# A first layer with half passes, a shorter lead, and f32 products in the last units

## The chip, the cores and the metric

The kernel runs on one core of one Trainium2 chip. The metric is the device time of a run in microseconds (us); lower is better. The engines are TensorE (PE in the profile; PEld is its weight load), VectorE (DVE), ScalarE (ACT), GpSimd (POOL) and SyncE (SP), which here only starts transfers.

## The reference, cut to what matters

```python
X = real(fft(fft(x, axis=1), axis=2))        # x: 8 x 3072 x 256 f32 -> 24576 tokens of 256
logits = X @ w_gate                          # 8 experts
e = argmax(logits, axis=1); gate = softmax(logits)[e]
ye = maximum(X @ w1[e], 0.0) @ w2[e]         # w1 256 x 1024, w2 1024 x 256, for each expert
X = gate * ye
h = X @ w_in                                 # 256 x 2048
P = a[0] + a[1]*h + a[2]*h**2 + a[3]*h**3
Q = 1.0 + abs(b[0])*abs(h) + abs(b[1])*h**2
out = (P / (Q + 1e-06)) @ w_out              # 2048 x 256, f32, 24576 x 256
```

With the inputs drawn, the experts get 3033, 3287, 3143, 2830, 2990, 2942, 3351 and 3000 tokens.

## The kernel before, in words

Three stages follow one another on the core.

*Transform, gate, scatter* (to about 350 us of the span). The two Fourier transforms are matrix products. Each token's expert, its place in that expert's list and its gate are found, and GpSimd scatters the token's row into `xs` in DRAM, sorted by expert (`scatter`, L610, 128 rows per indirect transfer). From the counts, VectorE computes tables for the first layer: which expert each pass has (`ej`), at which row its tokens start (`offi`), where its weights lie (`widx`), and a scale for each pass (`rj`, L990 to L993).

*First layer.* 103 passes (`NSB`) of 256 tokens, ordered by expert; each expert has as many whole passes as its tokens need. A pass loads 256 rows of `xs` (`load`, L1145), scales them and splits them into two f16 halves (`pairs`, L1151), transposes them (`transp`, L1167: on PE in the first ten passes, by DMA later), and has four pieces: `m1a` twice (the product with `w1`, 24 matmuls of 256 columns each, then ReLU on ACT and the rest of the f16 split on VectorE) and `m1b` twice (the product with `w2`, 24 matmuls). The weights of two passes lie in `wslot[0]` and `wslot[1]`; `gather` (L1004, an indirect transfer of 2 MB on POOL) loads them for pass j + 2, and moves nothing where the expert is the same. The result goes to `ys` in DRAM, in the sorted order, and the tokens' numbers to `idd`.

*Second layer.* 96 blocks of 256 tokens, four rational units each; the last unit is cut into two of half the width, so there are 385. A unit (j, u) has `m2a` (24 matmuls with `w_in`, then Abs, Square and Identity on ACT and the numerator, two operations, on VectorE: L1310 to L1315), `m2b` (Ln and Exp on ACT, L1322 and L1324, for the reciprocal of Q, and three operations on VectorE, L1325 to L1327), `m2g` (the product as two 16-bit halves `ghi` on ACT, L1335, and `glo` on GpSimd, L1336) and `m2c` (24 matmuls with `w_out`, L1348, into `po`; after a block's last unit it is scaled and scattered to the output). `bound_sum`, `bound`, `bound_scale` and `bound_out` work out scales for each block; `load_y` loads a block of `ys`.

The order of the work is written by hand: each engine runs its instructions in the order in which the code issues them. Lead: `np_` = 36 pieces without units, and beside each a `step` of a generator that prepares `w_in` and `w_out` (decode on VectorE, splits on ACT and GpSimd). Then one turn per unit i: `m2b` of unit i − 1, `m2a` of unit i, the piece i + `np_`, `m2g`, and `m2c` of unit i − 3. On PE that is m2a, a piece and m2c, three groups of 24 matmuls. Units 0 to 375 have a piece beside them; behind `free` = 4 · 103 − 36 = 376 there is none left.

## Time and profile before

| | us |
|---|---|
| median of 3 runs | 3513.91 (3513.57 to 3516.85) |
| profiled execution | 3516.32 |
| its span | 3514.6 |
| PE busy | 3391.1 (96%) |
| ACT busy | 3123.4 (89%) |
| DVE busy | 3044.7 (87%) |
| POOL busy | 2824.1 (80%) |

The span runs from the first to the last recorded instruction; 1.7 us of the profiled execution lie outside it. The mean granted clock of TensorE was 0.984 of full speed. The shares are averages over stages: in a table by windows, or in the chain of waits, each stage shows which engine sets its pace.

### The profile page before, as it was taken

What the parts mean: (1) busy time and instruction counts of PE and PEld (TensorE: products, weight loads), DVE (VectorE), ACT (ScalarE), POOL (GpSimd) and SP (SyncE); (2) the same over time, 40 slices, a digit from 0 to 9 for tenths busy, and PEclk for the clock granted to TensorE, in tenths of its full rate; (3) what the DMA queues carried; (4) which work ended last, traced back from release to release, by engine and by line L of the source; (5) the groups of instructions that cost most, each with busy time, mean ns of one, the idle gap of its engine ahead of it and who ended that gap; (6) DMA issues with size and microseconds to landing.
All of it is one profiled execution on the core that took longest, in us unless ns stands there. A gap on an engine that the chain in (4) does not pass through costs nothing.

```text
span 3514.6 us, 75025 instructions
## 1 busy us (share of the span) xinstructions
PE 3391.1 (96%) x29902; PEld 2968.8 (84%) x29902; DVE 3044.7 (87%) x3214; ACT 3123.4 (89%) x3904; POOL 2824.1 (80%) x2552
## 2 busy tenths in 40 slices
...
DMA packets 344639, 268.32 MB, mean 76 GB/s; under 512 B 182470, under 2 KB 319686, under 8 KB 337232
## 3 DMA queue, kind: packets, MB, share of 16 engines
...
q10 hardware_dynamic: 128, 1.06, 0.1%
...
## 4 chain that ended last, share of the span: by engine, by line
PE 88%; DVE 4%; ACT 2%; issue 2%; DMA 2%; POOL 1%; POOLq 0%; SPq 0%; ACTq 0%; DVEq 0%
PE po L1348 28%; PE h L1189 14%; PE h L1188 14%; PE h L1191 14%; PE py L1191 5%; PE py L1188 5%; PE py L1189 5%; POOL xs L612 1%; DMA xs<-y,sli 1%; PE ps L507 1%; PE pq L531 1%; PE ps L480 1%; PE pq L532 1%; DVE h L1326 0%; ACT h L1324 0%
## 5 line engine op out<-in xcount | busy, mean ns | idle before, releaser
L1188 PE MATMUL h<-yr,win 128*128 128x256 f16 x3072 | 755.7, 273 | 8.9 <-DVE u__5102 L1327 5.6
L1189 PE MATMUL h<-yr,win 128*128 128x256 f16 x3072 | 755.7, 273 | 0.0
L1348 PE MATMUL po<-wout,ghi 128*128 128x256 f16 x6144 | 735.1, 273 | 11.2 <-ACT ghi L1335 7.6
L1348 PEld LDWEIGHTS <-ghi 128*128 128x128 f16 x6144 | 593.6, 98 | 81.7 <-ACT ghi L1335 12.0
L1191 PE MATMUL h<-yr,win 128*128 128x256 f16 x3072 | 587.5, 273 | 0.0
L1324 ACT ACTIVATE h<-L,bnd 128x1024 f32<-128x1024 f32 x385 | 429.6, 1116 | 20.9 <-DVE u__47829 L1315 1.5
L1188 PE MATMUL h<-xt,wslot 128*128 128x256 f16 x1648 | 406.3, 274 | 2.5 <-DVE hlo L1214 1.7
L1189 PE MATMUL h<-xt,wslot 128*128 128x256 f16 x1648 | 406.3, 274 | 0.0
L1348 PE MATMUL po<-wout,glo 128*128 128x256 f16 x3072 | 399.3, 273 | 1.8 <-POOL glo L1336 1.8
L1188 PE MATMUL py<-hhi,wslot 128*128 128x256 f16 x1648 | 373.4, 274 | 3.5 <-ACT hhi L1208 3.5
L1189 PE MATMUL py<-hhi,wslot 128*128 128x256 f16 x1648 | 373.3, 274 | 0.0
L1189 PEld LDWEIGHTS <-wslot 128*128 128x128 f16 x3296 | 323.5, 98 | 45.1 <-issue 6.9
L1188 PEld LDWEIGHTS <-wslot 128*128 128x128 f16 x3296 | 323.3, 98 | 39.1 <-issue 0.4
L1191 PEld LDWEIGHTS <-wslot 128*128 128x128 f16 x3296 | 323.1, 98 | 38.5 <-issue 0.3
L1188 PEld LDWEIGHTS <-win 128*128 128x128 f16 x3072 | 300.7, 98 | 45.5 <-DVE u__5102 L1327 5.7
L1348 PEld LDWEIGHTS <-glo 128*128 128x128 bf16 x3072 | 300.4, 98 | 38.4 <-POOL glo L1336 3.2
L1189 PEld LDWEIGHTS <-win 128*128 128x128 f16 x3072 | 301.0, 98 | 35.2
L1191 PEld LDWEIGHTS <-win 128*128 128x128 f16 x3072 | 300.8, 98 | 35.2
L612 POOL DMA_INDIRECT xs<-y,sli x192 | 225.5, 1175 | 117.1 <-ACT L L535 58.5
L1191 PE MATMUL h<-xt,wslot 128*128 128x256 f16 x1648 | 315.8, 273 | 0.0
L1214 DVE SCALAR_TENSOR_TENSOR hlo<-h,hhi 128x1024 f16<-128x1024 f32 x197 | 240.0, 1218 | 29.1 <-ACT hhi L1208 24.1
L1361 POOL DMA_INDIRECT out_dram<-o,id x192 | 199.3, 1038 | 53.7 <-issue 47.3
...
## 6 DMA issues: line engine op xcount, KB each, us to landing
xr<-xs SPq DMA_DIRECT2D x103, 258.0 KB, 2.9
ys<-yw SPq DMA_DIRECT2D x103, 256.0 KB, 5.5
yr<-ys SPq DMA_DIRECT2D x96, 256.0 KB, 3.8
...
ws<-wh SPq DMA_DIRECT2D x16, 1024.0 KB, 12.1
...
```

The costliest lines, as they stand in the source:

```text
L480: nc.tensor.matmul(ps[0:m, 0:n], lhsT=eo[i][:, jh, c], rhs=mat[:, c, 0:n], start=c == 0, stop=c == 2)
L507: nc.tensor.matmul(ps[q][0:m, 0:NH], lhsT=eo[i][:, c], rhs=mat[:, c], start=c == 3 * q, stop=c == 3 * q + 2)
L531: nc.tensor.matmul(pq[:, k, 0:NC], lhsT=u[2 * par][:, js], rhs=rc, start=True, stop=False)
L532: nc.tensor.matmul(pq[:, k, 0:NC], lhsT=u[2 * par + 1][:, js], rhs=rs, start=False, stop=True)
L612: ins = nc.gpsimd.indirect_dma_start(out=xs, out_offset=bass.IndirectOffsetOnAxis(ap=sli[:, t0 + t:t0 + t + 1], axis=0), in_=y[:, t], in_o ...
L1188: nc.tensor.matmul(ps, lhsT=wa[i], rhs=xa[i], start=i == 0, stop=False)
L1189: nc.tensor.matmul(ps, lhsT=wb[i], rhs=xa[i], start=False, stop=False)
L1191: nc.tensor.matmul(ps, lhsT=wa[i], rhs=xb[i], start=False, stop=i == n - 1)
L1214: V.scalar_tensor_tensor(out=hlo[:, sl], in0=ps, scalar=0.0, in1=hhi[:, sl], op0=ALU.max, op1=ALU.subtract)
L1324: nc.scalar.activation(out=ps, in_=L, func=AF.Exp, scale=-1.0, bias=st["bnd", j][3])
L1348: nc.tensor.matmul(ps[:, q], lhsT=g[:, f - fs[0], q * P:(q + 1) * P], rhs=wout[:, h, 4 * u + f], start=g is ghi and u == 0 and f == 0 and ...
L1361: ins = nc.gpsimd.indirect_dma_start(out=out, out_offset=bass.IndirectOffsetOnAxis(ap=t[:, q:q + 1], axis=0), in_=o[:, q], in_offset=None, ...
```

## The change

1. The first layer gets `NF` = 95 passes of 256 tokens and nine *half passes* of 128. The tables for the half passes come from `half_tables`, run in three bursts in the turns of units 6, 14 and 22. A half pass has two pieces: `half_a` (48 matmuls of 128 columns) and both halves of `m1b` (48 matmuls of 128 columns). Where a pass of 256 tokens took four turns, a half pass takes two.
2. The lead has 24 pieces, with three steps of the preparation for two pieces. PE transposes serve the first 7 passes instead of 10. `load_y(0)` and the first bounds move along.
3. The load of the second weight slot and the operations for `rj` move behind the first loads of `xs`; the first pass is split by the gate scale in one operation per half instead of a multiply, a copy and a subtract; the edge tile scatters 8 rows instead of 128.
4. The units without a piece (375 to 384, `late`) issue `m2a` with `m2b` of the unit before between their own operations: Identity, the numerator, Abs, then `m2b`, then Square. Their product stays f32: no `ghi` and `glo`, and `m2c` has 8 matmuls in f32 with `w_out` widened to f32 into `wslot[0]` (`widen`).
5. `bound_sum` and `bound` run in turn u = 2 of a block instead of u = 1 where half passes stand (`at`).

The core of the diff:

```diff
+HB = TB // 2
...
-    NSB = NT // TB + E - 1
+    NF = NT // TB - 1
+    NSB = NF + E + 1
...
-        scatter(ye, sli, 0)
+        scatter(ye, sli, 0, B)
...
-        v = nc.sync.value_load(widx[0:1, 1:2], min_val=0, max_val=(E - 1) * P)
-        for h in range(2):
-            c = slice(4096 * h, 4096 * h + 4096)
-            nc.sync.dma_start(out=wslot[1][:, c], in_=ws[ds(v, P), c])
...
-        V.tensor_tensor(out=prod, in0=ej.unsqueeze(2).to_broadcast(bl),
-                        in1=sm[:, 8:16].unsqueeze(1).to_broadcast(bl), op=ALU.is_equal)
-        V.tensor_tensor(out=prod, in0=prod, in1=kk.unsqueeze(1).to_broadcast(bl), op=ALU.mult)
-        V.tensor_reduce(out=rj, in_=prod, axis=AX.X, op=ALU.add)
...
+    def full_scales():
+
+        bl = [P, NF, E]
+        t = tp.tile([P, 4, TB], F32, tag="u", name="rt").rearrange("p f t -> p (f t)")[:, 0:NF * E]
+        t = t.rearrange("p (j e) -> p j e", e=E)
+        V.tensor_tensor(out=t, in0=ej[:, 0:NF].unsqueeze(2).to_broadcast(bl),
+                        in1=sm[:, 8:16].unsqueeze(1).to_broadcast(bl), op=ALU.is_equal)
+        V.tensor_tensor(out=t, in0=t, in1=kk.unsqueeze(1).to_broadcast(bl), op=ALU.mult)
+        V.tensor_reduce(out=rj[:, 0:NF], in_=t, axis=AX.X, op=ALU.add)
...
+    def half_tables():
+
+        n = NSB - NF
...
+    def load_second(h):
+        c = slice(4096 * h, 4096 * h + 4096)
+        if h == 0:
+            st["w"] = nc.sync.value_load(widx[0:1, 1:2], min_val=0, max_val=(E - 1) * P)
+        nc.sync.dma_start(out=wslot[1][:, c], in_=ws[ds(st["w"], P), c])
...
+        if j == 0:
+            for i in range(n):
+                nc.scalar.activation(out=xp[:, i, 0], in_=t[:, i, 0:D], func=AF.Copy, scale=gs[:, i:i + 1])
+            for i in range(n):
+                V.scalar_tensor_tensor(out=xp[:, i, 1], in0=t[:, i, 0:D], scalar=gs[:, i:i + 1], in1=xp[:, i, 0],
+                                       op0=ALU.mult, op1=ALU.subtract)
...
-        if j < E + 2:
+        if j < LAG + 2:
...
+    def half_a(j):
+
+        W = wslot[j % 2]
+        xhi, xlo = [t[:, :, 0:HB] for t in st["xs", j]]
+        hhi = bp.tile([P, 8, TB], F16, tag="hhi", name="hhi")[:, :, 0:HB]
+        hlo = bp.tile([P, 8, TB], F16, tag="hlo", name="hlo")[:, :, 0:HB]
+        st["h", j] = (hhi, hlo)
+        ps = psM.tile([P, 4, TB], F32, tag="h1", name="h1").rearrange("p f (a t) -> p (f a) t", t=HB)
+        for f in range(8):
+            fo = f * P
+            three(ps[:, f], [W[:, kc * F1 + fo:kc * F1 + fo + P] for kc in range(2)],
+                  [W[:, 2048 + kc * F1 + fo:2048 + kc * F1 + fo + P] for kc in range(2)],
+                  [xhi[:, kc] for kc in range(2)], [xlo[:, kc] for kc in range(2)])
+        nc.scalar.activation(out=hhi, in_=ps, func=AF.Relu)
+        V.scalar_tensor_tensor(out=hlo, in0=ps, scalar=0.0, in1=hhi, op0=ALU.max, op1=ALU.subtract)
...
+        st["r", j, u, fs] = (ps, sq_, u_)
+
+        def numerator():
+            V.tensor_tensor(out=u_, in0=u_, in1=ps, op=ALU.mult)
+            V.scalar_tensor_tensor(out=u_, in0=u_, scalar=ka1, in1=ps, op0=ALU.add, op1=ALU.mult)
+
+        if between is not None:
+            nc.scalar.activation(out=u_, in_=ps, func=AF.Identity, scale=ka3, bias=ka2)
+            numerator()
         nc.scalar.activation(out=ab_, in_=ps, func=AF.Abs, scale=kb0)
+        if between is not None:
+            between()
         nc.scalar.activation(out=sq_, in_=ps, func=AF.Square, scale=kb1)
-        nc.scalar.activation(out=u_, in_=ps, func=AF.Identity, scale=ka3, bias=ka2)
+        if between is None:
+            nc.scalar.activation(out=u_, in_=ps, func=AF.Identity, scale=ka3, bias=ka2)
         (V if fs[0] else nc.gpsimd).tensor_tensor(out=sq_, in0=sq_, in1=ab_, op=ALU.add)
-        V.tensor_tensor(out=u_, in0=u_, in1=ps, op=ALU.mult)
-        V.scalar_tensor_tensor(out=u_, in0=u_, scalar=ka1, in1=ps, op0=ALU.add, op1=ALU.mult)
-        st["r", j, u, fs] = (ps, sq_, u_)
...
+    w32 = wslot[0].bitcast(F32)
+
+    def widen(q):
+        nc.gpsimd.tensor_tensor(out=w32[:, 1024 * q:1024 * q + 1024].rearrange("p (k d) -> p k d", d=D),
+                                in0=wout[:, 0, 4 * q:4 * q + 4], in1=wout[:, 1, 4 * q:4 * q + 4], op=ALU.add)
+
     def m2g(j, u, fs=range(4)):
         ps, q_, w_ = st.pop(("r", j, u, fs))
+        if 4 * j + u > free:
+            st["g", j, u, fs] = (w_, None)
+            return
...
+        if glo is None:
+            for f in fs:
+                k = (4 * u + f) * D
+                for q in range(2):
+                    nc.tensor.matmul(ps[:, q], lhsT=ghi[:, f - fs[0], q * P:(q + 1) * P], rhs=w32[:, k:k + D],
+                                     start=u == 0 and f == 0 and q == 0, stop=u == 3 and f == 3,
+                                     skip_group_check=True)
+        for g, parts in ((ghi, (0, 1)), (glo, (0,))) if glo is not None else ():
...
+        if i < 4 * NF:
+            j, s_ = divmod(i, 4)
+        else:
+            j, s_ = NF + (i - 4 * NF) // 2, (i - 4 * NF) % 2
+            if j >= NSB:
+                return
+            if s_ == 0:
+                pairs(j + 1, 1)
+                half_a(j)
+                if j + 1 < NSB:
+                    transp(j + 1)
+                if j + 3 < NSB:
+                    load(j + 3)
+            else:
+                m1b(j, 0, False)
+                m1b(j, 1, False)
+                pairs(j + 2, 0)
+                if j + 2 < NSB:
+                    gather(j + 2)
...
+    NB = NT // TB
+    LAG = E // 2 + 1
+    np_ = 24
+    free = 4 * NF + 2 * (NSB - NF) - np_
...
+    load_second(0)
     load_words(3, raw_in[1])
+    load_second(1)
...
+    gather(0)
     side = prologue()
+    late_tables = half_tables()
...
+    full_scales()
     load_words(5, raws[1])
 
-    NB = NT // TB
-    LAG = E
-    np_ = 4 * LAG + 4
     for i in range(np_):
-        if i == 4 * LAG:
+        if i == np_ - 4:
             load_y(0)
-        if i == 4 * LAG:
             bound_rows(0)
         piece(i, True)
-        step(1)
-        if i > 4 * LAG:
-            (bound_sum, bound, bound_scale)[i - 4 * LAG - 1](0)
+        step(2 - i % 2)
+        if i > np_ - 4:
+            (bound_sum, bound, bound_scale)[i - np_ + 3](0)
...
+    def at(i):
+        return 1 if i - i % 4 + 1 + np_ < 4 * NF else 2
...
+        late = free < i < len(units)
+        if 1 <= i <= len(units) and not late:
             m2b(*units[i - 1])
-        if i == len(units) - 1:
-            m2g(*units[i - lag])
         if i < len(units):
             j, u = units[i][:2]
             if i == 0:
                 piece(np_)
-            m2a(*units[i])
+            m2a(*units[i], between=(lambda: m2b(*units[i - 1])) if late else None)
             if i < len(units) - 1:
                 if i:
                     piece(i + np_)
-                if u == 1 and j + 1 < NB:
+                if u == at(i) and j + 1 < NB:
                     bound_sum(j + 1)
                 if u == 3 and j + 1 < NB:
                     bound_scale(j + 1)
                 if u == 1 and j + 1 < NB:
                     load_y(j + 1)
-        if i not in (free + 1, len(units) - 1, len(units)) and lag <= i < len(units) + lag:
+        if i not in (free + 1, len(units)) and lag <= i < len(units) + lag:
             m2g(*units[i - lag])
+        if free <= i < free + 4:
+            widen((i + 1) % 4)
...
+        if i % 8 == 6:
+            next(late_tables, None)
```

Two places show what moves in the engines' order, the first on two engines. On ScalarE, from the first units after the last piece. `ab`, `sq`, `u`, `L` and `h` are tiles of a unit, with a number for each; before:

```order
L1322 ACTIVATE L<-sq__47210,c1b 128x1024 [waits Pool_49]
L1324 ACTIVATE h_47184<-L,bnd 128x1024 [waits DVE_49,Activation_49]
L1310 ACTIVATE ab__47325<-h_47300,coef 128x1024 [waits PE_49]
L1311 ACTIVATE sq__47326<-h_47300,coef 128x1024
L1312 ACTIVATE u__47327<-h_47300,coef 128x1024
```

and now, for the unit with `h_47505` and the unit before it with `h_47436`:

```order
L1422 ACTIVATE u__47532<-h_47505,coef 128x1024 [waits PE_49]
L1424 ACTIVATE ab__47530<-h_47505,coef 128x1024 [waits DVE_49]
L1438 ACTIVATE L<-sq__47462,c1b 128x1024 [waits Pool_49]
L1440 ACTIVATE h_47436<-L,bnd 128x1024 [waits Activation_49]
L1427 ACTIVATE sq__47531<-h_47505,coef 128x1024
```

Abs (L1424) stands behind Identity and waits for VectorE; Exp (L1440) no longer does. On VectorE, in the same place of the changed program (the numerator is L1418 and L1419; L1441 to L1443 are those of `m2b`):

```order
L1441 SCALAR_TENSOR_TENSOR u__47389<-u__47389,a_3464,h_47362 128x1024 [waits Activation_49]
L1442 SCALAR_TENSOR_TENSOR h_47362<-sq__47388,h_47362 128x1024 [waits Pool_49]
L1443 SCALAR_TENSOR_TENSOR u__47389<-h_47362,bnd,u__47389 128x1024 [waits DVE_49]
L1418 TENSOR_TENSOR u__47532<-u__47532,h_47505 128x1024 [waits Activation_49]
L1419 SCALAR_TENSOR_TENSOR u__47532<-u__47532,coef,h_47505 128x1024 [waits DVE_49]
```

The value that Abs of `h_47505` waits for on VectorE is that of the last of these rows, the numerator of the same unit, and ahead of it stand the three operations of an earlier unit (`h_47362`). The other place is SyncE at the end of the scatter stage. Before, the two loads of the second weight slot (`wslot_70`; TENSOR_LOAD and ISA rows read an address for a transfer) stand ahead of the first load of `xs`:

```order
L951 DMA wslot_70<-ws 128x4096 [waits DMAHW4_49,DMAHW3_49,PE_49]
L951 ISA
L951 DMA wslot_70<-ws 128x4096 [waits DMAHW4_49,PE_49]
L1148 DMA xr<-xs 128x2x258 [waits DMASW4_49,DMASW5_49,DMASW3_49,DMASW6_49,DMASW2_49,DMASW7_49,DMASW1_49,DMAHW5_49,DMASW0_49,DMAHW7_49,DVE_49,Activation_49]
L1146 TENSOR_LOAD offi [waits DVE_49]
```

and now they stand behind the three loads of `xr`, of which the last is shown:

```order
L1218 DMA xr<-xs 128x2x258
L1224 TENSOR_LOAD widx
L1224 ISA x2
L1225 ISA
L1225 DMA wslot_70<-ws 128x4096
L225 DMA xh_68<-in_moe_w_in_dram 128x2048 [waits DVE_49]
```

The load of the slot no longer shares the transfer engines with the last scatters, and shares them with the loads of the word tiles `xh`.

## Rows read from the trace of the kernel before

**Rows 1.** The page, busy time of each engine, its share of the span and instructions.

```profile
PE 3391.1 (96%) x29902; PEld 2968.8 (84%) x29902; DVE 3044.7 (87%) x3214; ACT 3123.4 (89%) x3904; POOL 2824.1 (80%) x2552
```

**Rows 2.** Windows: length, busy time of the engines (instructions), granted clock, DMA share, GB/s.

```profile
2000.00:3000.00 1000.00, 1000.00 (x9210) 895.91 (x9209) 890.09 (x828) 945.25 (x1082) 839.34 (x766) 1.00 0.24 56
3485.00:3492.00 7.00, 5.53 (x27) 3.92 (x28) 5.68 (x6) 6.40 (x8) 6.51 (x5) 0.53 0.11 39
```

**Rows 3.** The chain of waits, 1000 to 1040 us: start, us, engine, tile and line.

```profile
1005.54 2.62 PE po L1348 x24
...
1013.40 2.62 PE po L1348 x24
```

**Rows 4.** The chain of waits at the boundary, 326 to 362 us.

```profile
343.88 5.78 DMA xs<-y,sli
...
352.86 0.70 DVE xr L1160
...
356.38 0.37 PE h L1188
```

**Rows 5.** Timeline of VectorE at the boundary: start, us, line, operation.

```profile
341.72 1.01 DVE L990 TENSOR_TENSOR blk<-tri,sm 128x832 f32<-128x832 f32 x1
...
343.82 1.02 DVE L993 TENSOR_REDUCE rj<-blk 128x104 f32<-128x832 f32 x1
```

**Rows 6.** Timeline of SyncE's queue, 336 to 338 us.

```profile
336.60 1.53 SPq L951 DMA_DIRECT2D wslot<-ws  x2
```

**Rows 7.** Timeline of PE at the end of the lead, 470 to 475 us.

```profile
474.43 0.27 PE L1188 MATMUL h<-yr,win 128*128 128x256 f16 x1
```

**Rows 8.** Waits of PE in the lead: total us, times, longest.

```profile
PE py L1188 <- ACT hhi L1208: 3.5, 2, 2.5
```

**Rows 9.** DMA issues in the lead: count, KB each, median us to landing.

```profile
wslot<-ws,widx POOLq DMA_INDIRECT x9, 10.8
```

**Rows 10.** The page, DMA issues of the whole span.

```profile
ys<-yw SPq DMA_DIRECT2D x103, 256.0 KB, 5.5
yr<-ys SPq DMA_DIRECT2D x96, 256.0 KB, 3.8
```

**Rows 11.** Timeline of PE, 364.4 to 365.2 us: transposes of 128 columns.

```profile
364.48 0.61 PE L1177 MATMUL pt<-ident,xp 128*128 128x128 f16 x8
364.93 0.27 PE L1188 MATMUL py<-hhi,wslot 128*128 128x256 f16 x1
```

**Rows 12.** Weight loads by line and shape: busy us, mean ns of one.

```profile
L1348 PEld LDWEIGHTS <-ghi 128*128 128x128 f16 x6144 | 593.6, 98 | 81.7 <-ACT ghi L1335 12.0 <-issue 0.9
```

**Rows 13.** Timeline of PE in the transform stage: f32 matmuls of 273 columns.

```profile
286.44 0.62 PE L531 MATMUL pq<-wslot,u 128*128 128x273 f32 x2
286.90 0.63 PE L532 MATMUL pq<-wslot,u 128*128 128x273 f32 x2
```

**Rows 14.** Timeline of ScalarE in the tail.

```profile
3419.96 1.12 ACT L1324 ACTIVATE h<-L,bnd 128x1024 f32<-128x1024 f32 x1
...
3450.63 1.12 ACT L1324 ACTIVATE h<-L,bnd 128x1024 f32<-128x1024 f32 x1 [0.60 <-DVE bnd L1287]
3451.68 1.09 ACT L1310 ACTIVATE ab__47476<-h,coef 128x1024 f32<-128x1024 f32 x1
...
3456.28 1.15 ACT L1322 ACTIVATE L<-sq__47477,c1b 128x1024 f32<-128x1024 f32 x1
3458.06 1.12 ACT L1324 ACTIVATE h<-L,bnd 128x1024 f32<-128x1024 f32 x1 [0.62 <-DVE u__47478 L1315]
...
3500.38 0.69 ACT L1324 ACTIVATE h<-L,bnd 128x512 f32<-128x512 f32 x1 [0.72 <-DVE u__47890 L1315]
```

**Rows 15.** Timeline of VectorE in the tail, 3440 to 3460 us.

```profile
3451.78 1.28 DVE L1325 SCALAR_TENSOR_TENSOR u__47395<-u__47395,a,h 128x1024 f32<-128x1024 f32 x1 [1.17 <-ACT h L1324]
...
3455.43 1.21 DVE L1314 TENSOR_TENSOR u__47478<-u__47478,h 128x1024 f32<-128x1024 f32 x1
3456.68 1.28 DVE L1315 SCALAR_TENSOR_TENSOR u__47478<-u__47478,coef,h 128x1024 f32<-128x1024 f32 x1
```

More of the change, by code (lines that the diff above doesn't have):

```diff
@@ L179, in fourier_moe_rational_kernel @@
     sx = keep.tile([P, 1], F32, name="sx")
+    ej = keep.tile([P, NSB], F32, name="ej")
+    oj = keep.tile([P, NSB], F32, name="oj")
+    tj = keep.tile([P, NSB], F32, name="tj")
+    hn = keep.tile([P, E], F32, name="hn")
+    ctok = keep.tile([P, E], F32, name="ctok")
+    cneg = keep.tile([P, E], F32, name="cneg")
+    cumx = keep.tile([P, E + 1], F32, name="cumx")
+    q9 = keep.tile([P, E + 1], F32, name="q9")
+    kk = keep.tile([P, E], F32, name="kk")
     nx2 = keep.tile([P, 1], F32, name="nx2")
@@ L940, in fourier_moe_rational_kernel @@
[L940 to L946 removed]
+        bl = [P, NF, E]
+        past = blk[:, 0:NF * E].rearrange("p (j e) -> p j e", e=E)
@@ L954, in fourier_moe_rational_kernel @@
         move = keep.tile([P, E], F32, name="move")
-        used = keep.tile([P, 104], F32, name="used")
-        V.tensor_scalar(out=used, in0=jrow, scalar1=cum[:, E - 1:E], scalar2=None, op0=ALU.is_lt)
+        used = keep.tile([P, NF], F32, name="used")
+        V.tensor_scalar(out=used, in0=jf, scalar1=cum[:, E - 1:E], scalar2=None, op0=ALU.is_lt)
         def places(k, end):
+            o = oj[:, 0:NF]
             V.tensor_tensor(out=prod, in0=past, in1=move.unsqueeze(1).to_broadcast(bl), op=ALU.mult)
-            V.tensor_reduce(out=oj, in_=prod, axis=AX.X, op=ALU.add)
-            V.scalar_tensor_tensor(out=oj, in0=jrow, scalar=float(TB), in1=oj, op0=ALU.mult, op1=ALU.add)
-            V.scalar_tensor_tensor(out=oj, in0=oj, scalar=-float(end), in1=used, op0=ALU.add, op1=ALU.mult)
-            V.tensor_scalar(out=offi[:, k], in0=oj[0:1], scalar1=float(end), scalar2=None, op0=ALU.add)
+            V.tensor_reduce(out=o, in_=prod, axis=AX.X, op=ALU.add)
+            V.scalar_tensor_tensor(out=o, in0=jf, scalar=float(TB), in1=o, op0=ALU.mult, op1=ALU.add)
+            V.scalar_tensor_tensor(out=o, in0=o, scalar=-float(end), in1=used, op0=ALU.add, op1=ALU.mult)
+            V.tensor_scalar(out=offi[:, k, 0:NF], in0=o[0:1], scalar1=float(end), scalar2=None, op0=ALU.add)
@@ L1143, in fourier_moe_rational_kernel, with tiles @@
     st = {}
+    def tiles(j):
+        return 2 if j < NF else 1
     def load(j):
-        rows = slice(0, TB) if j == 0 else ds(nc.sync.value_load(offi[0:1, 0, j:j + 1], min_val=0, max_val=E * R), TB)
-        t = bp.tile([P, 2, DX], F32, tag="xr", name="xr", bufs=4)
+        n = tiles(j)
+        rows = ds(nc.sync.value_load(offi[0:1, 0, j:j + 1], min_val=0, max_val=E * R), n * P)
+        t = bp.tile([P, 2, DX], F32, tag="xr", name="xr", bufs=4)[:, 0:n]
         nc.sync.dma_start(out=t, in_=xs[rows, :].rearrange("(t p) c -> p t c", p=P))
@@ L1179, in transp @@
             return
-        for q in range(2):
+        for q in range(tiles(j)):
             nc.sync.dma_start(out=xt.rearrange("p a k t -> p (a k) t")[:, :, q * P:(q + 1) * P],
@@ L1246, in bound_rows @@
         m = bp.tile([P, 2], F32, tag="ym", name="ym")
-        V.tensor_reduce(out=m, in_=ymx[:, :, j:min(j + E, NSB)], axis=AX.X, op=ALU.max)
+        end = j + LAG if j + LAG <= NF else min(NF + 2 * (j + LAG - NF) - 1, NSB)
+        V.tensor_reduce(out=m, in_=ymx[:, :, j:end], axis=AX.X, op=ALU.max)
         st["mm", j] = m2 = bp.tile([P, 2], BF16, tag="mm", name="mm")
```

132 lines of the change are left out of this document (91 added, 41 removed).

## The prediction

> **What bounds the kernel now.** The page first: the matrix engine (PE) is busy 3391.1 of 3514.6 us [rows 1]. So read stage by stage where it is not. In a window of the middle it is busy all the time [rows 2]; the chain of waits there runs through PE alone, one `po` group of 24 matmuls every 7.86 us [rows 3]. Such a turn is three groups of 24 (two of a unit, one first-layer piece), 2.62 us each, 0.109 us a matmul. Only work taken off PE, or moved where PE would idle, counts in the middle. PE is not full in three places: the boundary before the first first-layer matmul, the lead (37 pieces, to the first second-layer matmul), and the tail, the units without a piece beside them. The tail is bound by a loop over ACT and DVE, which the two timelines show [rows 14, 15].
>
> **The change, part by part.** The profiled execution (3516.32 us, of it 3514.6 span) is the base; it lies 2.4 us above the median of the runs, 3513.91, which I take off at the end.
>
> *Boundary.* The last scatter is issued at 343.88 and lands 5.78 us later; then come the load of `xr` and a short chain, and the first matmul at 356.38 [rows 4]. Two loads of 1 MB each into `wslot[1]` are issued at 336.60, beside the last scatters [rows 6]; the change puts them behind the three `xr` loads. With less traffic I take 2 us for the scatters' landing. Three operations for `rj`, from 341.72 to 344.75, leave VectorE's queue ahead of the word decoding [rows 5]; that ends nearly when `xr` lands, so with earlier data it would be late without this move. The multiply of piece 0, 0.70 us, goes from the chain [rows 4]; eight scattered rows instead of 128 for the edge tile save some more. I take −4.4 us; the ends are −2.5 (scatters bound as before) and −5. The cover of the `wslot[1]` load is now the first pass, 4 × 2.62 us; should it land later than that, the second pass starts late by as much.
>
> *Lead.* From 356.38 to 474.43 [rows 4, 7] it is 118.0 us. 37 × 2.62 = 96.9, nine sets of PE transposes at 0.45 [rows 11] make 4.0, and half clock at the start some 3 (the first 48 matmuls take from 356.38 to 364.48 [rows 4, 11], 8.1 instead of 5.2); 14 are stalls, such as `py` waiting for `hhi` [rows 8]. Now 25 pieces: 65.5, six sets of transposes 2.6, clock 3, is 71.1. The same preparation of the weights is squeezed in: 6 steps in 4 pieces, not 4. ACT's splits stand ahead of `hhi` more often, so the stalls grow: I take 18, ends 12 (less than now) and 24. Lead 89, so −29 (−35 to −23). The gain is real because pieces vanish: 412 before, 380 + 18 = 398 now, so PE has 14 × 2.62 = 36.7 us less work. Twelve of these are the shorter lead; the other two leave two more units at the end without a piece.
>
> *Turns with a piece.* Before they are units 0 to 375, now 0 to 373; same length. A half pass is 96 matmuls of 128 columns in two pieces. Eight transposes of 128 columns, each with a weight load of its own, begin at 364.48 and the next matmul at 364.93 [rows 11]: 0.45/8 = 0.056 us, half of 0.109, so a half piece costs 48 × 0.056 = 2.7 against 2.62, +1.5 us over 18. What runs once per pass now comes every 15.7 us (two turns) instead of 31.5. The drawn tokens leave six of the nine half passes used, each of another expert, so six gathers of 2 MB follow one another; in the lead such a transfer lands after 10.8 us [rows 9], and it has three turns less a group, some 21 us, until its weights are used. `ys` and `yr` take 5.5 and 3.8 [rows 10], the latter waiting on SyncE for the former, with the next `xr` behind it. I take +2 for the half stage, ends 0 and +10, and +1 (0 to +3) for the three bursts of small VectorE operations for the tables. Moving `bound_sum` to a later turn: nothing, its result is due two turns on; without that cover its small chain (under 1 us) would show.
>
> *Tail.* Before, the step from one exponential to the next is 3450.63 to 3458.06, 7.43 us [rows 14]: Exp 1.15, then VectorE's three operations on that unit from 3451.78 to 3455.43, 3.65, then the two of the next numerator, 2.5 [rows 15], then Exp again. The change puts the order on ACT as Identity(i), Abs(i), Ln(i−1), Exp(i−1), Square(i), and Abs(i) now waits for VectorE's numerator(i), as the order of the change shows. VectorE runs numerator(i+1) behind the three operations of unit i−1. The loop is then Exp 1.15 + 3.65 + 2.5 + Abs 1.0 + Ln 1.17 + 0.1 = 9.6 us per unit: Abs and Ln, which hid beside VectorE (Abs 3451.68 to 3452.68; Ln at 3456.28 [rows 14]), now lie in it. The step of rows 14 is 7.43, so +2.2 for each of seven steps (exponentials 375 to 382), 67.7 with 0.5 for small operations. The two steps before (373 to 375) contain m2a as well, as units 375 and 376 must wait until 373 and 374 have freed their product tile: 1.15 + 3.65 + 2.62 + Identity 1.1 (as wide as Abs) + 2.5 + 1.0 + 1.17 + starts 0.4 = 13.6 each. The last two steps (half-wide operations, such as the 0.69 of the last Exp [rows 14]) are 7.7 and 5.3, and from there to the end 14.2 as now. Sum 27.2 + 67.7 + 7.7 + 5.3 + 14.2 = 122.1, against 3514.6 − 3419.96 = 94.6 before [rows 14]: **+27**. Removed are the f16 copy of the product on ACT (as wide as Abs, some 1.0 us a unit) and its rest on GpSimd: worth nothing, as neither is in the loop. The f32 product: one f32 matmul of 273 columns is two records in the trace, and the next starts 0.46 us behind it [rows 13], so 0.43 for 256 columns; 8 × 0.43 = 3.45 against 2.62, hidden: PE needs 6.1 of 9.6 us. The cover has a limit: PE then has gaps of 3.5 us in each unit, and in a tail stretch where PE was not full (5.53 of 7 us) the clock was 0.53 [rows 2]; at the half level, 1.2 GHz, a unit would take 12.1. Low end +22, high end +33. The four `widen` operations on GpSimd go where its copies were: nothing.
>
> *Sum:* −4.4 − 29 + 1.5 + 2 + 1 + 27 = −1.9 → 3514.4 by the profiled execution; less 2.4, **3512 us**. The ends together: −5 − 35 + 22 = −18, and −2.5 − 23 + 10 + 3 + 33 + 1.5 = +22.
>
> **Rivals.** A measurement of this kernel can tell about 0.2%, 7 us, from no change.
>
> *Lead wins* (0.27): stalls in the lead stay at 12 to 14, the tail's loop is +22 to +25, the half passes cost nothing. For it: the stalls of before come from few places, and with fewer pieces some may vanish; against it, the splits of the weights stay as many. −4.4 − 34 + 1.5 + 1 + 23 = −13, 3501 us.
>
> *The numerator's wait doesn't bind* (0.08): if Abs finds its numerator done, VectorE's five operations set the step, 3.65 + 2.5 = 6.15. Then 7 × (9.6 − 6.15) = 24 and some 12 in the first two steps go from the sum: 3512 − 36 = 3476 us. Against it: the numerator stands directly behind the three operations that wait for Exp.
>
> *SyncE's queue is late in the half stage* (0.20): `ys` 5.5, `yr` 3.8 and the load and transposes behind them fit 15.7 us as they are, but next to 2 MB gathers they may take half as long again. 5.5 + 3.8 + some 3 for `xr` and as much for the transposes is 15.3; half again is 23, over by 7, on the four or so half passes that meet a `yr`: 29, less the 2 counted, 3539 us; over by 3 it is 3522. It decides as soon as the sum passes 15.7.
>
> *Weight loads bound 128 columns* (0.05): a load takes 98 ns [rows 12]; if two can't overlap, 864 matmuls cost 98 and not 56 ns: +36, 3547 us. Against it are eight transposes in a row at 56 [rows 11]. The Trainium skill (TensorE: Matmul & The Clock Gate, section "Back-to-back issue gap") states about 81 ns per matmul for a sustained stream of weight load and matmul pairs at 128 columns. By that rule 864 matmuls would cost 22 us more, an estimate: 3533 us. The trace has only short rows of eight at 56, so it speaks against the rule but shows no sustained stream.
>
> **How the numbers follow.** The forecast, no change to be told, 0.40; lead wins 0.27; no binding wait 0.08; late queue 0.20; weight loads 0.05. Faster 0.35, same 0.40, slower 0.25. The range 3497 to 3533 has the ends of the sum (3494 to 3536), less a little, and leaves out the wait that doesn't bind (0.08), the weight loads (0.05) and the worst of the queue (some 0.07): 0.2. The likeliest case's own range is 3507 to 3520.
>
> **What would show it.** First m1a at 352 instead of 356.4; first second-layer matmul near 441 instead of 474.4; exponentials of late units 9.6 us apart, with Abs idle behind a VectorE numerator; 7.86 us a turn in the half stage; 128-column matmuls 0.056 apart. Exponentials 6.2 or 7.4 apart would break the tail's term; a lead of 77 or 100 us the lead's; a PE wait for `xt` or `wslot` in the half stage would be the late queue.

## The result, and the profile after

The changed kernel took 3534.4 us (median of 5 runs, 3533.81 to 3537.58) against 3515.84 for the kernel before beside it: ratio 1.0054, 95% interval 1.0043 to 1.0065. It is slower, by 0.54%; 3512 and no change were forecast, and the range ended at 3533. The profiled execution has a span of 3532.6 us, 18.0 more than before. Of the runs below, four single ones took 3957 us and more (one of half_split, one of lead36, two of best2), and medians and ratios leave them out.

The page of the kernel after, busy time of each engine (against [rows 1]):

```profile
PE 3373.8 (96%) x29902; PEld 2952.9 (84%) x29902; DVE 3045.4 (86%) x3248; ACT 3102.8 (88%) x3887; POOL 2801.2 (79%) x2549
```

PE has 17 us less work, ACT 21 and POOL 23, and the kernel is longer; nothing here says where. A table by stage does. It is worked out from the first matmuls in PE's timeline (of `m1a`, of `m2a`) and the starts of Exp in ScalarE's, one for each unit; the last column ends with the span.

| us | first m1a at | lead | units 0 to 24 | 352 to 373 | 373 to 375 | 375 to 382 | 382 to end |
|---|---|---|---|---|---|---|---|
| before | 356.4 | 118.1 | 188.0 | 165.2 | 15.8 | 52.3 | 26.5 |
| after | 350.7 | 99.6 | 190.7 | 178.5 | 29.8 | 65.5 | 25.9 |
| difference | −5.7 | −18.5 | +2.7 | +13.3 | +14.0 | +13.2 | −0.6 |

The units 24 to 352 agree within 0.4 us. The half passes stand beside units 356 to 373. The rows behind the table, from PE's timeline of the kernel after (columns as in [rows 7]):

```profile
350.70 0.37 PE L1274 MATMUL h<-xt,wslot 128*128 128x256 f16 x1 [0.78 <-DVE xt L1264]
...
450.31 0.27 PE L1274 MATMUL h<-yr,win 128*128 128x256 f16 x1
```

and from ScalarE's timeline of the kernel after, units 352, 373, and two of the tail with the Abs between them (against [rows 14]):

```profile
3232.93 1.12 ACT L1440 ACTIVATE h<-L,bnd 128x1024 f32<-128x1024 f32 x1
...
3411.47 1.12 ACT L1440 ACTIVATE h<-L,bnd 128x1024 f32<-128x1024 f32 x1 [0.41 <-DVE u__47167 L1419]
...
3450.79 1.12 ACT L1440 ACTIVATE h<-L,bnd 128x1024 f32<-128x1024 f32 x1
...
3458.22 1.11 ACT L1424 ACTIVATE ab__47601<-h,coef 128x1024 f32<-128x1024 f32 x1 [4.19 <-DVE u__47603 L1419]
3459.24 1.14 ACT L1438 ACTIVATE L<-sq__47531,c1b 128x1024 f32<-128x1024 f32 x1
3460.41 1.12 ACT L1440 ACTIVATE h<-L,bnd 128x1024 f32<-128x1024 f32 x1
```

ScalarE stands idle for 4.19 us ahead of this Abs, until VectorE has the numerator; Ln and Exp follow it. From Exp to Exp it is 9.6 us, as forecast. The lead and the stretch with half passes are the two places where the sum went wrong. The waits of PE, of the kernel after, first in the lead, then from 3270 to 3412 us (line and tile that waited, what for: total us, times, longest):

```profile
PE pm L1360 <- DVE xt L1264: 5.5, 1, 5.5
PE py L1277 <- DVE hlo L1300: 4.9, 2, 3.0
PE py L1274 <- ACT hhi L1294: 2.5, 1, 2.5
PE topb L1062 <- DVE xt L1264: 2.5, 1, 2.5
PE topt L1057 <- DVE xt L1264: 2.5, 1, 2.5
```

```profile
PE h L1274 <- DMA yr<-ys: 3.6, 1, 3.6
PE h L1274 <- DVE ymx L1332: 1.9, 1, 1.9
PE h L1274 <- DVE u__46905 L1443: 1.8, 1, 1.8
PE py L1275 <- issue: 1.5, 2, 0.8
```

In the lead of before there were 3.5 us for `hhi` [rows 8] and some 2 each for two others; the list is now longer, and the rows shown all name work on ACT and VectorE. In two windows of the lead of the kernel after (columns as in [rows 2]) PE works half of the time, and in the second the granted clock is 0.72:

```profile
386.00:398.00 12.00, 6.41 (x57) 5.31 (x56) 9.53 (x10) 9.59 (x10) 11.00 (x13) 0.96 0.38 60
434.00:446.00 12.00, 6.15 (x39) 4.60 (x40) 1.82 (x2) 6.83 (x9) 11.29 (x14) 0.72 0.20 45
```

In the first, `hlo` stands at 394.7 behind an operation of the decode on VectorE, and VectorE had waited 2.4 us for GpSimd just before. The second is the end of the lead: ACT runs the splits of `w_out` one behind the other, and the ReLU of the pass (`hhi`) stands behind them. The longest wait of the list, 5.5 us, bears VectorE's name but begins there, as the timelines of ACT, VectorE and PE show together:

```profile
436.37 1.06 ACT L1077 ACTIVATE wout<-wo 128x1024 f16<-128x1024 f32 x1
437.33 1.01 ACT L1294 ACTIVATE hhi<-h 128x1024 f16<-128x1024 f32 x1
438.37 1.23 DVE L1300 SCALAR_TENSOR_TENSOR hlo<-h,hhi 128x1024 f16<-128x1024 f32 x1 [8.16 <-ACT hhi L1294]
439.51 0.68 DVE L1264 COPY xt<-pt 128x1024 f16<-128x1024 f16 x1
440.24 0.19 PE L1360 MATMUL pm<-mm,ones 128*128 128x1 bf16 x2 [5.53 <-DVE xt L1264]
```

### The profile page after: what moved, and what is told of

Its sections match the earlier page's. It is cut to its first block, busy times and chain, and to the rows that moved or that the text cites. A ratio compares the mean times of both kernels' runs of the same rounds, so it can differ in the third digit from the quotient of the medians.

```text
span 3532.6 us, 75024 instructions
## 1 busy us (share of the span) xinstructions
PE 3373.8 (96%) x29902; PEld 2952.9 (84%) x29902; DVE 3045.4 (86%) x3248; ACT 3102.8 (88%) x3887; POOL 2801.2 (79%) x2549
## 4 chain that ended last, share of the span: by engine, by line
PE 81%; DVE 6%; ACT 4%; issue 3%; POOL 3%; DMA 3%; SPq 0%; POOLq 0%; DVEq 0%; ACTq 0%
PE po L1480 26%; PE h L1274 13%; PE h L1275 13%; PE h L1277 13%; PE py L1277 5%; PE py L1274 5%; PE py L1275 5%; POOL xs L626 2%; DMA xs<-y,sli 1%; ACT h L1440 1%; DVE h L1442 1%; PE ps L521 0%; PE ps L494 0%; ACT L L1438 0%; DMA idd<-xr 0%
## 5 line engine op out<-in xcount | busy, mean ns | idle before, releaser
L1274 PE MATMUL h<-yr,win 128*128 128x256 f16 x3072 | 758.3, 274 | 29.4 <-DVE u__47305 L1443 8.4
L1480 PE MATMUL po<-wout,ghi 128*128 128x256 f16 x6000 | 717.0, 273 | 3.9 <-ACT ghi L1460 3.9
L1480 PEld LDWEIGHTS <-ghi 128*128 128x128 f16 x6000 | 579.4, 98 | 70.5 <-ACT ghi L1460 4.2
L1440 ACT ACTIVATE h<-L,bnd 128x1024 f32<-128x1024 f32 x385 | 429.6, 1116 | 16.9 <-DVE u__5348 L1419 0.4
L1274 PE MATMUL h<-xt,wslot 128*128 128x256 f16 (+1 forms) x1664 | 398.3, 269 | 3.3 <-DVE hlo L1300 2.4
L1275 PE MATMUL h<-xt,wslot 128*128 128x256 f16 (+1 forms) x1664 | 398.2, 269 | 0.0
L1480 PE MATMUL po<-wout,glo 128*128 128x256 f16 x3000 | 389.0, 273 | 0.6 <-POOL glo L1461 0.6
L1274 PE MATMUL py<-hhi,wslot 128*128 128x256 f16 (+1 forms) x1664 | 365.0, 270 | 2.5 <-ACT hhi L1294 2.5
L1275 PE MATMUL py<-hhi,wslot 128*128 128x256 f16 (+1 forms) x1664 | 365.3, 270 | 1.5 <-issue 1.5
L1277 PE MATMUL h<-xt,wslot 128*128 128x256 f16 (+1 forms) x1664 | 310.9, 269 | 0.0
L1300 DVE SCALAR_TENSOR_TENSOR hlo<-h,hhi 128x1024 f16<-128x1024 f32 x184 | 224.1, 1218 | 11.5 <-ACT hhi L1294 11.5
```

The costliest lines, as they stand in the source:

```text
L1274: nc.tensor.matmul(ps, lhsT=wa[i], rhs=xa[i], start=i == 0, stop=False)
L1275: nc.tensor.matmul(ps, lhsT=wb[i], rhs=xa[i], start=False, stop=False)
L1277: nc.tensor.matmul(ps, lhsT=wa[i], rhs=xb[i], start=False, stop=i == n - 1)
L1300: V.scalar_tensor_tensor(out=hlo[:, sl], in0=ps, scalar=0.0, in1=hhi[:, sl], op0=ALU.max, op1=ALU.subtract)
L1440: nc.scalar.activation(out=ps, in_=L, func=AF.Exp, scale=-1.0, bias=st["bnd", j][3])
L1480: nc.tensor.matmul(ps[:, q], lhsT=g[:, f - fs[0], q * P:(q + 1) * P], rhs=wout[:, h, 4 * u + f], start=g is ghi and u == 0 and f == 0 and ...
```

## The experiments

The theory after the result had three parts: the order of the late units (Abs waits), the lead (the same preparation beside fewer pieces), and the half stage (transfers). The runs t_ring, tables, best and best2 were made where every kernel's transform stage was some 30 us longer, so of them the ratios and the stages from the first `m1a` on are read, not the times. The kernel before was run beside each. In lead36 the half passes stand beside earlier units (from 344 on), so the column of units 352 to 373 is left open. How much a stage varies from run to run can be read down a column: the runs whose lead is that of the changed kernel have 97.0 to 100.9 us there.

| kernel | median | ratio to before (interval) | lead | units 0 to 24 | 352 to 373 | 373 to 375 | 375 to 382 |
|---|---|---|---|---|---|---|---|
| t_abs | 3512.78 | 0.9985 (0.9976 to 0.9995) | 99.0 | 190.6 | 180.7 | 24.6 | 47.2 |
| t_old | 3513.75 | 0.9989 (0.9979 to 0.9998) | 97.0 | 190.5 | 182.6 | 19.5 | 52.1 |
| t_ring | 3538.80 | 0.9971 (0.9947 to 0.9994) | 99.0 | 190.8 | 181.9 | 21.2 | 47.2 |
| lead_steps | 3532.97 | 1.0043 (1.0029 to 1.0057) | 96.1 | 190.9 | 182.7 | 29.4 | 65.5 |
| lead36 | 3521.11 | 1.0011 (1.0001 to 1.0021) | 123.9 | 190.3 | – | 14.3 | 44.8 |
| half_yr | 3535.61 | 1.0050 (1.0033 to 1.0066) | 100.2 | 190.7 | 179.1 | 29.5 | 65.5 |
| half_gather | 3545.39 | 1.0078 (1.0061 to 1.0095) | 100.9 | 190.7 | 187.0 | 29.0 | 65.5 |
| half_split | 3542.46 | 1.0067 (1.0047 to 1.0087) | 98.6 | 191.0 | 188.1 | 30.0 | 65.5 |
| half_nogather | 3529.06 | 1.0029 (1.0016 to 1.0042) | 100.7 | 190.7 | 175.8 | 29.5 | 65.5 |
| tables | 3568.35 | 1.0044 (1.0021 to 1.0068) | 98.9 | 193.8 | 180.3 | 28.9 | 65.5 |
| best | 3538.62 | 0.9968 (0.9946 to 0.9990) | 95.0 | 193.9 | 199.3 | 20.9 | 47.2 |
| best2 | 3535.27 | 0.9977 (0.9964 to 0.9989) | 95.0 | 190.4 | 181.5 | 21.0 | 47.2 |

### The tail

**t_abs**

```diff
             nc.scalar.activation(out=u_, in_=ps, func=AF.Identity, scale=ka3, bias=ka2)
-            numerator()
         nc.scalar.activation(out=ab_, in_=ps, func=AF.Abs, scale=kb0)
         if between is not None:
+            numerator()
             between()
```

> Edit: in the units without a piece Abs stands ahead of the numerator, so that Abs no longer waits for VectorE; Square then does. Theory (the wait of Abs puts Abs and Ln into the loop): the step between exponentials falls from 9.55 us to VectorE's five operations, 6.2 to 6.6, on seven to eight steps, and the kernel gains 22 to 28 us, to about 3509 us, below the 3516 of before. Rival (the f32 products bind: PE needs 2.6 + 3.45 us a unit, 12 at half clock): the step stays at 8 us or more and the gain is under 12 us.

One line moved, and 3512.78 us instead of 3534.4: the step is 47.2/7 = 6.74 us, and the gain 21.6 us, each a little short of the theory and far from the rival. ScalarE's timeline of t_abs:

```profile
3451.78 1.10 ACT L1423 ACTIVATE ab__47601<-h,coef 128x1024 f32<-128x1024 f32 x1
3452.77 1.14 ACT L1438 ACTIVATE L<-sq__47531,c1b 128x1024 f32<-128x1024 f32 x1
3453.95 1.12 ACT L1440 ACTIVATE h<-L,bnd 128x1024 f32<-128x1024 f32 x1
3455.54 1.11 ACT L1427 ACTIVATE sq__47602<-h,coef 128x1024 f32<-128x1024 f32 x1 [0.47 <-DVE u__47603 L1419]
```

Abs and Ln follow at once, and the wait for the numerator, now in front of Square, is 0.47 us. Of the 21.8 us between the two profiles' spans these seven steps give 18.3.

**t_old**

```diff
-        if 1 <= i <= len(units) and not late:
+        if 1 <= i <= len(units):
             m2b(*units[i - 1])
...
-            m2a(*units[i], between=(lambda: m2b(*units[i - 1])) if late else None)
+            m2a(*units[i])
```

> Edit: in the units without a piece the order of the kernel before (m2b of the unit before, then Abs, Square, Identity, numerator), with the f32 products kept. Theory (the order makes the loop, the f32 products and the missing 16-bit halves are beside it): the step is 7.4 us as in the kernel before, the kernel gains 14 to 18 us to about 3518. Rival (the f32 products cost PE time that counts): the step is 8 us or more.

The step is 52.1/7 = 7.44 us, that of before, with the f32 products. So the order alone made the step of the changed kernel, 65.5/7 = 9.4 us on the mean, and the f32 products cost nothing to be seen in the step. The kernel gained 20.7 us, more than the 14 to 18 expected. Against t_abs the longer steps lose 4.9 us, but units 373 to 375 are 5.1 us shorter, and the two kernels are not told apart (0.9985 and 0.9989).

**t_ring**

```diff
-        own = i < 1 or i % 3
+        own = i < 1 or i % 3 != 1
```

> Edit, against t_abs: the product tiles of the late units take turns so that the first late unit gets the tile that the first layer no longer uses, and each later one that of three units before. Theory (the first two late units wait for a tile of two units before: PE 5.9 us for one of them, then at half clock): exponentials 373 to 375 go from 24.6 us to 14 to 17, the kernel gains 7 to 10 us against t_abs. Rival (the start of the tail is bound by ACT and VectorE finishing the units with pieces): 22 us or more, under 3 us gained.

21.2 us instead of 24.6 for units 373 to 375, between the two expectations: the wait for a tile was a part, not most. In t_abs PE waited for it in `m2a`:

```profile
PE h L1274 <- DVE u__47305 L1443: 5.9, 1, 5.9
```

### The lead

**lead_steps**

```diff
-        step(2 - i % 2)
+        step((0, 2, 2, 2)[i % 4])
```

> Edit: the six preparation steps of four pieces are given as 0, 2, 2, 2 instead of 2, 1, 2, 1, so that none stands between the two ReLUs of a pass on ACT. Theory (the lead's extra 10 us are ACT's splits ahead of hhi): PE's waits at 390 us (3.0) and 434 to 440 us (5.5 and the half clock behind it) shrink, the lead falls from 99.6 us to 86 to 92, and the kernel gains 8 to 13 us. Rival (VectorE is full in the lead, with the decode ahead of hlo and xt): the lead changes by less than 4 us either way.

The rival held: 96.1 us, 3.5 less, which is hardly more than the lead varies from run to run, and the kernel the same within its interval (1.0029 to 1.0057). The waits for `hhi` are gone, but PE now waits for `xp`, of GpSimd and of ACT. PE's waits in the lead of lead_steps:

```profile
PE pt L1263 <- POOL xp L1251: 5.2, 3, 2.5
PE pt L1263 <- ACT xp L1250: 3.2, 1, 3.2
```

So it is not one place in the queue: cured there, the waits appear at other work beside the preparation.

**lead36**, against t_abs:

```diff
-    np_ = 24
+    np_ = 36
...
-        step(2 - i % 2)
+        step(1)
```

> Edit, against t_abs: 36 pieces in the lead with one preparation step each, as before, so 12 more units at the end without a piece. Theory (the lead's stalls come from squeezing the same preparation into fewer pieces): the lead is 37 pieces in 117 to 119 us, 14 to 16 us of stalls instead of 28; the 12 more units cost 6.7 us without a piece where a turn took 7.87 with one and PE needs 6.1; sum against t_abs: 14 less stall, 12 x 0.6 = 7 more gaps, so 3 to 9 us gained. Rival (the stalls belong to the number of pieces with PE transposes or to the earlier start): the stalls stay at 25 or more and the kernel loses 5 us or more.

A miss: 3521.11 us, 8 us slower than t_abs. The lead is 123.9 us; 37 × 2.62, six sets of transposes and 3 for the clock are 102.5, so stalls of 21.4, against 27.9 in t_abs and 14 before. PE's waits in it:

```profile
PE h L1274 <- DMA xt<-xp: 5.8, 2, 3.2
PE py L1274 <- ACT hhi L1294: 4.9, 5, 2.5
```

With one step for a piece the stalls of before come back (`hhi`), and 5.8 us of others come with DMA transposes in the lead, which the kernel before did on PE up to pass 10. So of the 14 us of extra stalls in t_abs the squeezing explains 27.9 − 21.4 = 6.5 by that count, and some 12 if the waits for the DMA transposes, which are new in the longer lead, are set aside. The count is good to a few us, as the lead varies by 4. That the short lead is worth its stalls here is shown by the same run: with the long one the kernel is slower.

### The half stage

**half_yr**

```diff
-                if u == 1 and j + 1 < NB:
+                if u == (1 if at(i) == 1 else 0) and j + 1 < NB:
                     load_y(j + 1)
```

> Edit: where half passes stand, load_y is issued at turn u = 0 of a block, ahead of the write of ys in turn u = 1, instead of right behind it. Theory (SyncE waits for that write, which the gather holds up, before it can go on to yr, the transposes and xr): the waits for yr (3.6 us and the half clock behind it) and those of 1.9 and 1.8 us in the half stage go, and the kernel gains 8 to 12 us. Rival (the extra work per pass on ACT, VectorE and GpSimd makes the half stage long): under 3 us.

No gain: 179.1 us. SyncE's queue of half_yr shows why, and behind it a row of its waits from 3270 to 3412 us:

```profile
3274.55 0.65 SPq L1343 DMA_DIRECT2D yr<-ys  x1
3275.31 0.56 SPq L1345 DMA_DIRECT2D id<-idd  x1
3284.76 0.60 SPq L1336 DMA_DIRECT2D ys<-yw  x1
```

```profile
SPq L1336 <- DMA yr<-ys: 13.4, 3, 8.1
```

`yr` is issued early, and then the queue stands for 9.5 us all the same, of which 8.1 are the write of `ys` waiting until `yr` has landed; the transposes behind it are late instead (PE waits 4.1 us for `xt`). So the order on SyncE alone is not the cause: here the load of `yr`, issued 0.8 us behind a gather (3273.72, on POOL), takes some 10 us, against a median of 3.8 [rows 10], and the next transfer on SyncE waits for it. In the kernel after, too, a gather of 2 MB is issued just ahead of a slow transfer:

```profile
3308.78 1.10 POOL L1011 DMA_INDIRECT wslot<-ws,widx  x1 [0.22 <-issue]
```

```profile
3309.75 0.61 SPq L1336 DMA_DIRECT2D ys<-yw  x1
3310.53 0.48 SPq L1338 DMA_DIRECT2D idd<-xr  x1
3321.61 0.64 SPq L1343 DMA_DIRECT2D yr<-ys  x1
```

11.1 us lie between `idd` and `yr`, which waits for the write of `ys`; the median of a `ys` write was 5.5 [rows 10].

**half_gather**

```diff
                 if j + 3 < NSB:
                     load(j + 3)
+                if NF < j < NSB - 1:
+                    gather(j + 1)
             else:
...
                 pairs(j + 2, 0)
-                if j + 2 < NSB:
-                    gather(j + 2)
```

> Edit: where half passes stand, the gather of weights is issued a turn later, behind the write of ys on the transfer engines, not ahead of it. Theory (the 2 MB gather fills the transfer engines ahead of the ys write): ys lands in 3 to 6 us instead of 11, the next yr is issued in time, and the kernel gains 6 to 12 us, unless the gather itself is now late for its weights, which would show as a wait of PE for wslot. Rival (the load of yr is late because it stands behind ys in SyncE's queue whatever the gather does): under 3 us.

The other way: 187.0 us, and PE waits for `yr`, 11.6 us in two pieces. The time of the gather matters; that it now meets the other transfers of the half pass is the likely reason, but not shown.

**half_split**: two gathers of 1 MB, of the rows of `ws` seen as two half rows each, with an index table for them (two more small operations).

```diff
+                if j + 2 < NSB:
+                    gather_part(j + 2, 0)
             else:
...
                 if j + 2 < NSB:
-                    gather(j + 2)
+                    gather_part(j + 2, 1)
```

> Edit: where half passes stand, the gather of a pass's weights is two of 1 MB, w1 behind half_a and w2 behind m1b, a turn apart, in place of one of 2 MB. Theory (each 2 MB gather fills the transfer engines for 8 to 10 us, and whatever SyncE issues behind it, ys, yr, xr or a transpose, waits that long): the longest such delay halves to 4 to 5 us, PE's waits for yr, xt and hlo in the half stage mostly go, and units 352 to 373 take 167 to 172 us instead of 178.5; 7 to 11 us gained. Rival (the stage is long for its extra work on ACT, VectorE and GpSimd, not for transfers): 176 us or more, under 3 us gained.

Slower, 188.1 us. It did not do what it was made for: in the DMA view of a stretch of 100 us (3268 to 3368) the gathers' queue, which also carries the scatters to the output, moves as much, in 1.6 times the engines' time. First the kernel after, then half_split (packets, MB, share of 16 engines):

```profile
q0 software_dynamic: 1152, 9.18, 31.7%
```

```profile
q0 software_dynamic: 1765, 8.83, 51.0%
```

So the two theories are not told apart by it; it only shows more time on the transfer engines and a longer stage together.

**half_nogather, ring_nogather and ring_nogather_2** leave out the gathers from the third half pass on, four of the six, with the edit below; these passes then use an earlier expert's weights, so their output is another. The second and third are one kernel, t_ring with that edit:

```diff
                 pairs(j + 2, 0)
-                if j + 2 < NSB:
-                    gather(j + 2)
```

> Edit: no gather of weights from the third half pass on; these passes use the weights of an earlier expert, so their output differs. Theory (the gathers' traffic): units 352 to 373 take 166 to 169 us instead of 178.5, with no wait of PE for yr, xt or ymx. Rival (extra work per pass): 175 us or more.

> Edit: t_ring, and no gather of weights from the third half pass on (these passes use an earlier expert's weights, so their output differs). Theory (the gathers are most of the half stage's loss, the stall without a releaser in half_nogather was a chance one): units 352 to 373 take 167 to 171 us, against 181.9 in t_ring and 175.8 in half_nogather. Rival (the half passes cost 10 us by themselves, through more instructions and more work per pass): 174 to 178 us again, with stalls that name no releaser or VectorE.

> The same kernel once more. Theory: 167 to 171 us again, or a chance stall at another place; rival: 174 to 178 us with the same stalls at the same places.

Units 352 to 373 took 175.8 us, in the rival's range, and then 173.2 and 172.8 us, between theory and rival; the last two kernels took 3499.1 and 3501.6 us in one run each, against 3515.9 for the kernel before. PE's waits from 3225 to 3410 us, first in ring_nogather, then in ring_nogather_2:

```profile
PE py L1274 <- issue: 1.3, 1, 1.3
...
PE h L1274 <- DVE u__45746 L1443: 1.0, 1, 1.0
```

```profile
PE h L1274 <- DMA yr<-ys: 1.6, 1, 1.6
PE h L1274 <- DVE u__46884 L1443: 1.0, 1, 1.0
```

The large wait for `yr` is gone. The eight kernels with all gathers at their place take 178.5 to 182.7 us, so a difference of 3 or 4 us between two single profiles says little. The four gathers cost 2.7 us by half_nogather against the kernel after, and 9 us by the two ring_nogather runs against t_ring; 8 to 11 us over before remain without them.

Most of that remainder can be read from the traces. ScalarE's Ln now waits for GpSimd's sum (`sq`, L1430) once in a block of four units: four times, 2.5 or 2.6 us each, in ring_nogather_2 from 3225 to 3410 us and also in the kernel after, and never in that stretch of before. ScalarE's first wait in ring_nogather_2, then GpSimd's timeline of ring_nogather ahead of such a sum (of the seven small operations of `bound`, L1372, the first and the last), with the Ln that waits for it on ScalarE:

```profile
ACT L L1438 <- POOL sq__45165 L1430: 2.6, 1, 2.6
```

```profile
3347.98 0.29 POOL L1372 TENSOR_SCALAR bnd<-bnd,scal 128x1 f32<-128x1 f32 x1
...
3350.51 0.29 POOL L1372 TENSOR_SCALAR bnd<-bnd 128x1 f32<-128x1 f32 x1
3351.29 1.08 POOL L1493 DMA_INDIRECT out_dram<-o,id  x1 [0.48 <-issue]
...
3353.68 2.36 POOL L1430 TENSOR_TENSOR sq__46325<-sq__46325,ab__46324 128x1024 f32<-128x1024 f32 x1
```

```profile
3356.08 1.15 ACT L1438 ACTIVATE L<-sq__46325,c1b 128x1024 f32<-128x1024 f32 x1 [1.97 <-POOL sq__46325 L1430]
```

`bound` and the two scatters to the output stand one behind the other, ahead of the sum, since part 5 of the change put `bound` into turn u = 2, the turn of the scatters. Before, it stood a turn ahead of them:

```profile
3358.10 0.29 POOL L1267 TENSOR_SCALAR bnd<-bnd,scal 128x1 f32<-128x1 f32 x1
...
3365.85 1.10 POOL L1361 DMA_INDIRECT out_dram<-o,id  x1 [0.18 <-issue]
```

In ring_nogather the chain of waits from 3318 to 3400 us runs through GpSimd, ScalarE and VectorE and not through PE. From one block's scatter to the next it is 33.2 us there (3318.11 to 3351.29), and 31.5 before (3334.34 to 3365.85); PE's own work for four such turns is 31.7. 1.7 us a block is some 7 or 8 us over the four and a half blocks with half passes, about what remains. No run put `bound` back into its old turn, so its share is worked out and not tested.

### The tables, and a kernel that is faster

**tables**: the operations of half_tables in some twenty bursts of one to three, one in each turn from unit 6.

```diff
-        if i % 8 == 6:
+        if i >= 6:
             next(late_tables, None)
```

> Edit, against the changed kernel: the tables of the half passes in some twenty bursts of one to three operations from unit 6 on, not in three bursts of about ten. Theory (a burst on VectorE is longer than the slack of a turn, the same operations one by one are not): the first 24 units take 197 us as before, not 199.4; 2 to 3 us gained in the kernel. Rival (the operations cost their time however they are spread): no gain.

No gain, as the rival had it, and even a loss: 193.8 us for the first 24 units, against 190.7 with three bursts. PE's waits in these units are all for VectorE, which was busy 182.7 us with its 186 operations there, against 176.5 with three bursts. Why the same operations take longer when they are spread was not looked into.

**best** (t_ring, lead_steps and the spread tables), **best2** (without the spread):

> Edit: t_ring, with the steps of lead_steps and the spread tables. If the parts add up: t_abs 3512.8, less 7 to 10 for the tiles, 1 to 3 for the lead and 2 to 3 for the tables, so 3497 to 3503, some 15 us (0.4%) below the kernel before. Rival (what one part frees, the next stage takes): above 3508.

> Edit: t_ring with the steps of lead_steps, and the tables of the half passes in three bursts as in the changed kernel. If the parts add up: against the kernel before t_abs stood at 0.9985, the tiles give 3 to 4 us in units 373 to 375 and the steps 3 to 4 us in the lead: 0.996 to 0.9975 of the kernel before. Rival (the half stage, which is late by transfers, takes back what comes early): 0.998 or more.

best2 is 0.9977 of the kernel before (0.9964 to 0.9989), best 0.9968 (0.9946 to 0.9990). Both beat the kernel before, by a quarter of a per cent, but neither is told apart from the other, from t_ring alone (0.9971) or from t_abs (0.9985). best2 lies between its theory and its rival, and the 0.996 that the parts of best promised is within its interval; in the profile of best, which was its slowest run, the half stage took 199.3 us, with one wait of 12.6 us for `xt`.

## Why the prediction was wrong, point by point

- *Boundary:* −4.4 forecast (−2.5 to −5), −5.7 measured. A little better than its better end; in the eight other runs of the table above that lack the longer transform stage the first `m1a` is at 350.2 to 353.0, so the term was right.
- *Lead:* −29 forecast (−35 to −23), −18.5 measured. The step that failed is "the stalls grow: I take 18, ends 12 and 24". They are 99.6 − 71.1 = 28.5. The mechanism was named, ACT's splits ahead of `hhi`, but the term looked at `hhi` alone. PE's waits for it are 2.5 us; 4.9 us for `hlo` and 10.5 for `xt` on VectorE came on top, 5.5 of them behind the splits of `w_out` at the end of the lead, and behind that the granted clock is 0.53 from 440 to 445 us. lead_steps shows that one of them cured brings out another, lead36 that one step for a piece takes half of the growth or more back.
- *Half stage:* +3.5 forecast with the half pieces (ends to +11.5), +13.3 measured. The half pieces themselves were right: from 3318.72, the first of 48 matmuls of 128 columns in `m1b`, to the next group at 3321.40 it is 2.68 us, 0.056 us each. PE's timeline of the kernel after:

```profile
3318.72 0.22 PE L1274 MATMUL py<-hhi,wslot 128*128 128x128 f16 x1
...
3321.40 0.60 PE L1480 MATMUL po<-wout,ghi 128*128 128x256 f16 x4
```

  By the rule of the Trainium skill (TensorE: Matmul & The Clock Gate, section "Back-to-back issue gap") 48 would take 3.9 us at 81 ns each, an estimate. This run of 48, each with a weight load of its own, does not agree, and the measurement decides.

  What failed is "I take +2 for the half stage", 11.8 by measurement. Two steps are in it. The slack of each transfer was counted alone, not six gathers of 2 MB beside the others: leaving out four of them gives 3 to 9 us back. And "moving `bound_sum` to a later turn: nothing, its result is due two turns on" looked at when the result is due and not at what stands behind it on GpSimd: its seven operations and the scatters hold up the sum that Ln waits for, some 7 or 8 us by the count above.

  The rival "SyncE's queue is late" (0.20, 3522 to 3539) had the place, and its mechanism, the chain on SyncE slowed by the gathers, is a part of it; GpSimd it did not have. That the measured time lies in its range is in part luck: 13.3 us in the half stage belongs to its lower end, 3522, and the rest of the way comes from the lead.
- *Tables:* +1 forecast (0 to +3), +2.7 measured, near the worse end.
- *Tail:* +27 forecast; 373 to the end took 121.2 us against 94.6, +26.6. Six of the seven steps were 9.5 to 9.6 us as forecast, the seventh 8.1; units 373 to 375 took 29.8 where 27.2 were counted: PE stood for 8.4 us, and from 3425.2 to 3441.2 us the granted clock was 0.70 (a limit that the prediction names). The seven steps took 65.5 where 67.7 were counted, and what follows them 25.9 where 27.2 were, so the close sum owes something to errors that cancel. t_abs shows that the wait was its cause, t_old that the f32 products cost nothing.

Terms of 3532.6 − 3514.6 = 18.0: −5.7 − 18.5 + 2.7 + 13.3 + 14.0 + 13.2 − 0.6 = 18.4, less 0.4 in the units between. Against the sum of the prediction, −1.9, the lead is 10.5 off and the half stage 9.8, in the same direction, and no other term by more than 1.7. (Two small slips in the prediction's arithmetic change nothing: its lower end, 18 us below 3513.9, is 3496 and not 3494, and 36 us above 3512 is 3548 and not 3547.)

## What to carry to other kernels

Where less work is put beside the same preparation, count the stalls from every queue that the preparation shares, not from the one in which a wait shows now: cured at one place, the wait can come back at the next. A half-size piece halves the matmuls but not its weights, so count the transfers of all its neighbours together. When an operation moves to a later turn, look at what it now stands ahead of on its own engine, even where that engine has time to spare on the mean. Read the order of an edited loop for waits between two readers of one tile: here one line moved by one place was 22 us.

## What had not been expected

- Two gathers of 1 MB from half rows took more of the transfer engines' time than one of 2 MB: 51.0% against 31.7% of a 100 us stretch, for 8.83 and 9.18 MB on that queue.
- Some twenty short bursts on VectorE cost more than three longer ones: 5.8 us over before in the first 24 units, against 2.7.
- In the half stage PE stood for up to 2.2 us without a releaser in the profile (half_nogather), which was not seen in that stretch before; its cause is open.
